# Batch 0's low-rank mixing in four partial sums at full array height, 58 instead of 62 unread matmuls, batch 1's values in two parts

## The chip, the cores and the metric

One core of a Trainium2 chip. The metric is the device time of one execution in microseconds (us), median over repeated executions. TensorE is called PE, its weight loads PEld, VectorE DVE, ScalarE ACT, GpSimd POOL, SyncE SP, as in the profile.

## The reference

Sliding-window attention with a window of 64 over 8 batches, 8 heads, 576 positions, 64 dimensions; then a token mixing of rank 32 and an MLP:

```python
scores = np.where(mask, scale * np.matmul(q, k.transpose(0, 1, 3, 2)), -1e9)   # window 64
x = softmax(scores) @ v                      # heads side by side: [8, 576, 512]
u = x + ((x.transpose(0, 2, 1) @ U) @ V).transpose(0, 2, 1)     # rank 32
out = u + np.maximum(u @ w_ch1, 0.0) @ w_ch2                    # 512 -> 2048 -> 512
```

## The kernel before

One instruction stream per engine. While the MLP of one chunk of 512 tokens runs on PE (`psA` is its first layer, `psU` its second), pieces of the next batches' attention are put between its matmuls at slots of a table. Four places matter here. The start keeps PE busy while the first inputs load, with matmuls whose results nobody reads ("unread"):

```python
def turn_over(n, cols, rows=P):
    for _ in range(n):
        nc.tensor.matmul(unread[0:rows, 0:cols], idle[:, 0:rows], idle[:, 0:cols], start=True, stop=True)
turn_over(62, 96)
```

Each of these pairs is a weight load and a matmul, two PE instructions. Then batch 0's attention: transposes of k and q (`tpm`, `tpg`), scores (`sc`), values (`xh`, `xr`), and its mixing. `UM` makes x U in four groups of 32 output rows, `HT` and `VM` multiply by V:

```python
for g in (t % 2, t % 2 + 2):                                  # UM, steps t = 0 to 3
    nc.tensor.matmul(hh["ps"][g * R : (g + 1) * R, :], ub[odd][:, t, :], xt, start=(t < 2), stop=False)
...
half = slice(n * 2 * R, (n + 1) * 2 * R)                      # VM: 64 of the 128 rows
nc.tensor.matmul(ps[0][n], vrep[half, off : off + P], hh["sb"][half, lo : lo + cols], start=True, stop=True)
```

Batch 1's values (`PVA`) are one piece of 72 matmuls at slot 20. VectorE then normalises them (`xs`), and batch 1's mixing (`pshh`) at slot 25 waits for that. The second weight matrix `w2b` is loaded in four quarters. Batch 0 has `spare=True`, the others not.

The softmax here doesn't subtract the row's maximum and nothing guards it: scores larger than these inputs give would overflow.

## Time and profile before

| | before |
|---|---|
| median of three executions | 312.85 us (312.75 to 312.92) |
| the profiled execution | 313.08 us, span 311.4 us |
| PE busy | 98% of the span |
| batch 0's U, last step / first `psA` of its MLP | 19.21 / 21.80 us |
| batch 1's mixing starts | 51.61 us |
| last quarter of `w2b` lands | 47.7 us |

The times within the span are read from the timeline of PE. After batch 1's mixing PE runs through almost without a wait, so a shift of PE at 51.61 us is a shift of the end, unless something later takes it back.

### The profile page before, as it was taken

To read this page: it belongs to the slowest core of one execution; us is meant where nothing else is said; L and a number is where in the kernel's file an instruction comes from. 1 tells how busy PE (TensorE), PEld (TensorE's weight loads), DVE (VectorE), ACT (ScalarE), POOL (GpSimd) and SP (SyncE) were. 2 spreads that over 40 slices of the span, in tenths; PEclk is the share of its full clock that TensorE was granted. 3 is DMA by queue.
4 is the path that set the end of the run, shared out by engine and by line. 5 is a ranking of instruction groups with operands and counts; after the bars stand their busy time and mean duration, and the time that the engine had idled before them with its cause. 6 is when DMAs were issued, how large, how long until landed. Compare 5 with 4: busy or idle time off the path is not lost.

```text
span 311.4 us, 6970 instructions
## 1 busy us (share of the span) xinstructions
PE 303.9 (98%) x2897; PEld 148.4 (48%) x2919; DVE 161.8 (52%) x308; ACT 108.8 (35%) x173; POOL 101.7 (33%) x133
## 2 busy tenths in 40 slices
PE   8989999999999999999999999999999999999996
PEld 7643554544455544453445344544454444444443
DVE  4665467437758753774368435844574343016011
ACT  3745670467038510642063304340345003201500
POOL 8693263293497097029308710000000000000000
PEclk9999999999999999999999999999999999999999
DMA  7999999999999999999999999515100545010012
GB/s 108 167 210 208 205 168 147 145 148 154 129 150 140 126 152 156 182 161 159 163 155 207 150 106 181 128 48 133 69 2 0 120 180 193 27 76 34 0 64 73
DMA packets 156496, 39.88 MB, mean 128 GB/s; under 512 B 145040, under 2 KB 151440, under 8 KB 156464
## 3 DMA queue, kind: packets, MB, share of 16 engines
q0 software_dynamic: 104720, 18.88, 87.3%
q1 hardware_dynamic: 51744, 20.55, 35.0%
q8 instruction: 23, 0.38, 0.5%
q14 instruction: 9, 0.07, 0.1%
HBM read 37.97 MB, written 9.44 MB: 152 GB/s over the span
## 4 chain that ended last, share of the span: by engine, by line
PE 93%; DMA 3%; POOL 2%; issue 1%; ACT 0%; DVE 0%; POOLq 0%
PE psA L724 41%; PE psU L748 40%; DMA vA<-in_v_dram 3%; PE sc L345 3%; PE xw L407 2%; PE psv L619 2%; PE pshh L531 1%; PE tpu L653 1%; PE tpg L281 0%; POOL qr L119 0%; PE low L345 0%; PE psh L531 0%; POOL vB L151 0%; PE xr L407 0%; POOL kr L119 0%
## 5 line engine op out<-in xcount | busy, mean ns | idle before, releaser
L724 PE MATMUL psA<-uTc,w1b 128*128 128x512 bf16 (+1 forms) x580 | 131.2, 378 | 0.4 <-ACT uTc L599 0.4
L748 PE MATMUL psU<-w2b,c 128*128 128x512 bf16 (+2 forms) x572 | 127.5, 373 | 1.3 <-issue 0.3
L748 PEld LDWEIGHTS <-c 128*128 128x128 bf16 x592 | 56.0, 98 | 66.4 <-issue 3.6
L724 PEld LDWEIGHTS <-w1b 128*128 128x128 bf16 x580 | 54.1, 98 | 64.4 <-issue 2.9
L736 ACT ACTIVATE c<-psA 128x512 bf16<-128x512 f32 x84 | 50.0, 597 | 88.3 <-PE psA L724 88.0
L761 DVE TENSOR_TENSOR osb<-psU,un 128x512 f32<-128x512 f32 (+2 forms) x29 | 19.5, 672 | 69.3 <-PE psU L748 69.3
L734 DVE TENSOR_SCALAR c<-psA 128x512 bf16<-128x512 f32 x60 | 41.3, 688 | 25.6 <-PE psA L724 25.6
L634 DVE TENSOR_TENSOR un<-psv,xs 128x512 bf16<-128x512 f32 (+3 forms) x48 | 26.1, 592 | 23.5 <-PE psv L619 23.3
L365 ACT ACTIVATE pts<-sc 128x1024 bf16<-128x1024 f32 x32 | 31.4, 1028 | 2.3 <-PE sc L345 2.3
L137 POOL DMA_DIRECT2D vA<-in_v_dram x32 | 28.5, 915 | 8.1 <-DMA w1b<-in_moe_w_ch_dram 2.8
L128 POOL DMA_DIRECT2D qr<-in_q_dram x30 | 26.7, 890 | 4.5 <-DMA w2b<-in_moe_w_ch_dram 3.1
L128 POOL DMA_DIRECT2D kr<-in_k_dram x30 | 26.7, 890 | 4.1 <-PE psA L724 2.0
L398 ACT ACTIVATE ptl<-low 128x256 bf16<-128x256 f32 x6 | 2.3, 384 | 62.0 <-PE high L345 62.0
L371 DVE TENSOR_TENSOR pts<-pts,maskA 128x1024 bf16<-128x1024 bf16 x28 | 19.1, 682 | 1.7 <-ACT pts L365 1.7
L922 POOL COPY held<-qf 1x1 bf16<-1x1 bf16 x5 | 1.1, 228 | 54.0 <-DMA qf<-qr 54.0
L498 DVE TENSOR_TENSOR xs<-xw,rcw 128x896 bf16<-128x896 f32 x14 | 15.3, 1091 | 0.5
L345 PEld LDWEIGHTS <-kf 64*64 64x64 bf16 x704 | 9.9, 107 | 7.7 <-issue 7.0
L345 PE MATMUL sc<-qf,kf 64*64 64x128 bf16 (+1 forms) x608 | 11.7, 212 | 0.5 <-DVE qf L298 0.3
L407 PEld LDWEIGHTS <-pts 128*64 128x64 bf16 x512 | 9.9, 110 | 3.7 <-issue 3.2
L546 ACT CAST hh<-pshh 128x512 bf16<-128x512 f32 x7 | 4.1, 586 | 13.7 <-PE pshh L539 13.5
L656 ACT COPY uTc<-tpu 128x512 bf16<-128x512 bf16 x9 | 5.3, 585 | 10.2 <-PE tpu L653 10.2
L407 PE MATMUL xw<-vA,pts 128*64 128x65 bf16 x217 | 8.4, 195 | 0.0
(115 smaller groups left out, 175.3 us busy)
## 6 DMA issues: line engine op xcount, KB each, us to landing
out_dram<-osb SPq DMA_DIRECT2D x27, 256.0 KB, 2.3
vA<-in_v_dram POOLq DMA_DIRECT2D x32, 128.0 KB, 8.1
kr<-in_k_dram POOLq DMA_DIRECT2D x24, 128.0 KB, 5.8
qr<-in_q_dram POOLq DMA_DIRECT2D x24, 128.0 KB, 6.4
w2b<-in_moe_w_ch_dram POOLq DMA_DIRECT2D x4, 512.0 KB, 15.0
out_dram<-late SPq DMA_DIRECT2D x8, 256.0 KB, 3.0
vB<-in_v_dram POOLq DMA_DIRECT2D x8, 128.0 KB, 12.3
w1b<-in_moe_w_ch_dram POOLq DMA_DIRECT2D x2, 512.0 KB, 11.5
```

Source lines behind the costliest of these rows:

```text
L128: nc.gpsimd.dma_start(out=dst[0:rows, t, :, :], in_=src[b, :, t * P : t * P + rows, :].rearrange("h p d -> p h d"),)
L137: nc.gpsimd.dma_start(out=dst[:, :, 0:D], in_=v[b, :, lo : lo + P, :].rearrange("h p d -> p h d"))
L345: nc.tensor.matmul(sc[g][r0 : r0 + W, col * W : (col + n) * W], keys_of(j, u, rs), queries_of(j, blk, n, rs), start=not spare, stop=last o ...
L365: nc.scalar.activation(out=dst, in_=sc[:], func=ACT.Exp, scale=scale)
L371: nc.vector.tensor_tensor(out=dst, in0=dst, in1=maskA.rearrange("p g n w -> p g (n w)"), op=ALU.mult)
L407: nc.tensor.matmul(dst, pts[:, h // 2, h % 2, blk, :] if blk < NB - 1 else ptl[:, h // 2, h % 2, :], rhs, start=True, stop=True,)
L634: nc.vector.tensor_tensor(out=u_tiles[g][rs, cs], in0=ps[0][n][rs], in1=x[rs, t, :, :].rearrange("p h d -> p (h d)")[:, cs], op=ALU.add,)
L724: nc.tensor.matmul(ps[i][:, ts.start * P : ts.stop * P], w1b[:, dc, i * P : (i + 1) * P], uTc[:, ts, dc, :], start=(dc == 0), stop=(dc == ...
L734: nc.vector.tensor_relu(out=c1[i][:], in_=ps[i][:])
L736: nc.scalar.activation(out=c1[i][:], in_=ps[i][:], func=ACT.Relu)
L748: nc.tensor.matmul(acc[t][:, lo:hi], c1[i][:, t * P : (t + 1) * P], w2b[:, i, lo:hi], start=(i == 0), stop=(i == NFC - 1),)
L761: nc.vector.tensor_tensor(out=osb[:, lo:hi], in0=acc[t][:, lo:hi], in1=u_tiles[g][:, lo:hi], op=ALU.add,)
```

## The change

It is a local tuning of three places: batch 0's mixing gets matmuls of full array height in place of pairs of small tiles, the start gets fewer unread matmuls of slightly more columns, and batch 1's values are cut in two so that VectorE can begin to normalise sooner. The core of the diff, with cuts:

```diff
-    turn_over(62, 96)
+    turn_over(58, 102)
...
-                        for g in (t % 2, t % 2 + 2):
+                        for g in (t,) if spare else (t % 2, t % 2 + 2):
-                                start=(t < 2), stop=False,
+                                start=(t < 2 or spare), stop=False,
...
-                        cols = slice((g % 2) * CH // 2, (g % 2 + 1) * CH // 2)
+                        n = NFULL if spare else 2
+                        cols = slice((g % n) * CH // n, (g % n + 1) * CH // n)
...
-                        hh["sb"][half, dc * P : (dc + 1) * P],
-                        vrep[half, W : W + CH],
+                        hh["sb"][:, dc * P : (dc + 1) * P],
+                        vrep[:, W : W + CH],
...
-                    half = slice(n * 2 * R, (n + 1) * 2 * R)
+                    half = slice(0, P) if spare else slice(n * 2 * R, (n + 1) * 2 * R)
...
-        pcs["PV"] = [PVA] if not spare else ...
+        pcs["PV"] = [PVA] if b > 1 else [lambda: PVA((0,), False), lambda: PVA((1,))] if b == 1 else ...
...
-        "SV": [18, 18, 19, 19],
-        "PV": [20],
+        "SV": [18, 18, 19, 21],
+        "PV": [20, 22],
```

Inside `PVA` the loops over `n` now run over the part's `ns`, and the tail (`rest`, `one`) belongs to the second part. I call the three parts the start, the mixing and the split.

## The prediction

> **What bounds the kernel now.** I read the page first: who is busy, and what the chain that ended last is made of.
>
> ```profile
> span 311.4 us, 6970 instructions
> PE 303.9 (98%) x2897; PEld 148.4 (48%) x2919; DVE 161.8 (52%) x308; ACT 108.8 (35%) x173; POOL 101.7 (33%) x133
> ...
> PEclk9999999999999999999999999999999999999999
> DMA  7999999999999999999999999515100545010012
> ...
> PE 93%; DMA 3%; POOL 2%; issue 1%; ACT 0%; DVE 0%; POOLq 0%
> ```
>
> TensorE (PE) is busy 98% of the span at full granted clock, and 93% of the chain is PE. What is not PE is 3% DMA, 2% POOL and 1% issue, near the start. Next the table of who waited for whom on PE; it is seven rows long, and these are the ones inside the parts that change:
>
> ```profile
> PE unread L829 <- DVE idle L155: 1.3, 1, 1.3
> PE psA L724 <- ACT uTc L599: 0.4, 1, 0.4
> PE psh L539 <- issue: 0.4, 1, 0.4
> PE psU L748 <- issue: 0.3, 2, 0.2
> ```
>
> All seven add up to 3.1 us, 1.0% of 311.4. So the change, which touches three short places (the start, batch 0's mixing, batch 1's values), is about tenths of a microsecond; 2% would be 6.3 us. To place the tenths I read the timeline of PE around these places.
>
> ```profile
> 1.26 5.03 PE L829 MATMUL unread<-idle 128*128 128x96 bf16 x62 [1.26 <-DVE idle L155]
> ...
> 19.21 0.39 PE L531 MATMUL psh<-xs,ub 128*32 128x512 bf16 x2
> 19.97 0.29 PE L539 MATMUL psh<-xs,ub 128*32 128x256 bf16 x4 [0.36 <-issue]
> ...
> 21.80 1.89 PE L724 MATMUL psA<-uTc,w1b 128*128 128x512 bf16 x8 [0.40 <-ACT uTc L599]
> 23.62 0.39 PE L619 MATMUL psv<-hh,vrep 64*128 64x512 bf16 x2
> 23.94 1.04 PE L724 MATMUL psA<-uTc,w1b 128*128 128x512 bf16 x4
> ...
> 46.96 0.29 PE L407 MATMUL one<-vA,pts 128*64 128x65 bf16 x8
> 47.41 4.26 PE L748 MATMUL psU<-w2b,c 128*128 128x512 bf16 x19 [0.16 <-issue]
> 51.61 0.62 PE L531 MATMUL pshh<-xs,ub 128*32 128x512 bf16 x8
> ```
>
> Batch 1's values run from 45.90 (their first row) to 47.06 (start of the last), 72 matmuls at 16.4 ns, then second-layer matmuls (psU), then batch 1's mixing (pshh) at 51.61. The 0.16 us of idle before psU at 47.41 is probably not real: the weight loads restart at 47.18, and the page counts 22 fewer matmuls than loads, so a first psU at 47.20 is missing from the records. Two more lines matter, from the timeline of POOL and the table of DMA issues of 34 to 40 us: the last quarter of the second weight matrix.
>
> ```profile
> 35.68 0.75 POOL L243 DMA_DIRECT2D w2b<-in_moe_w_ch_dram  x1 [1.17 <-DMA w2b<-in_moe_w_ch_dram]
> ...
> w2b<-in_moe_w_ch_dram POOLq DMA_DIRECT2D x1, 512.0 KB, 12.0
> ```
>
> It lands at 35.68 + 12.0 = 47.7, with the DMA engines at 9 in all slices since about 8 us. Its issue waited for an earlier transfer, not for PE. This is a clock that does not move when PE gets faster.
>
> **What the Trainium skill says.** "TensorEngine Tiling (Array Packing)", Key Properties: changing the tiling mode, not merely the tile, drains TensorE. The trace agrees: a full-height 512-column matmul takes 13.81/64 = 0.216 us in the long psA runs, but the stretch from 21.80 to the psA at 27.28 holds 20 psA and three 64-row groups and takes 5.48 us; 5.48 - 20 x 0.216 = 1.17 us for the three groups, which concurrent matmuls of 512, 512 and 256 columns would fill for only 0.54. "TensorE: Matmul & The Clock Gate", Part 3, says tiles in different row or column groups run concurrently, some 4 ns apart. The trace agrees: the pairs of 32-column matmuls (L531) cover 0.39 us, one psU 0.38. Part 1 of that page says the clock is halved until about 3.4 us of sustained work. The trace shows 62 matmuls of 96 columns at 80 ns (4.96/62), and 96-column transposes at about 40 ns a pair right after 6.22: the switch falls just where these matmuls end. "Runtime: NRT & Kernel Launch", Instruction fetch mechanics, says instructions come in 16 KiB blocks of 256, mostly hidden; the page's 23 instruction packets of 0.38 MB agree in size, no view ties a wait to one.
>
> **The change part by part.**
>
> Start: 62 x 96 becomes 58 x 102 columns, 5952 becomes 5916. At 80 ns per 96 columns (0.83 ns each) that is 0.03 us less. It is worth nothing: the chain here runs through the load of v to 14.0 us and POOL's copies to 16.07. Eight instructions fewer, though.
>
> Batch 0, U: five steps. In four, two concurrent matmuls become one; since the second was free, about 0. In the last, four concurrent matmuls go from 256 to 128 columns: 128/512 x 0.216 = 0.05 us saved, on the path (it leads to hh, uTc, and the first psA at 21.80). HT: two concurrent pairs become four in turn; the first psA waits only for the copy of the first, so 0. The 0.36 us of issue before L539 (0.43 after what a normal follow-on would be, since 19.21 + 0.32 = 19.53) is not explained by its semaphore: the DVE result was ready at 19.2. If it is an instruction block arriving, the 16 instructions fewer before it move it to a place where PE waits for ScalarE anyway, and up to 0.43 us is won.
>
> Batch 0, V: three groups at 1.17 us become 4 x 0.216 + 2 x 0.109 = 1.08: 0.09 us saved. Sum of the front, called G: 0.14 us, or 0.57 if the issue wait goes.
>
> Batch 1's values: 28 matmuls at 45.90 - G, then 4 psU, then 4 psU that are the first to use the last quarter of w2b, then the other 44 values, then 12 psU, then the mixing. Before, all 72 stood ahead, so those psU ran at 47.20 + 4 x 0.216 = 48.06, 0.3 us after the landing. Now they are reached at 45.90 - G + 28 x 0.0164 + 0.12 (return to the full array, 47.06 + 0.016 to 47.20) + 0.86 = 47.34 - G, which is before 47.7. So PE waits until about 47.78, whatever G is. From there: 4 psU 0.86, switch 0.09, 44 values 0.72, switch 0.12, 12 psU 2.59, switch 0.09: mixing could start at 52.25, against 51.61, that is +0.64.
>
> VectorE adds to this. Before, its normalising took from 47.17 to 51.34 (4.2 us) and PE came at 51.61. Now one of the two large pieces (0.26 + 1.01 us) runs early, but the rest, 0.21 + 0.35 + 0.26 + 1.01 + 0.20 + 0.86 = 2.89 us, starts only after the second part. PE's stretch from the last value matmul to the mixing shrinks from 4.55 to 4.55 - 8 x 0.216 = 2.82, so PE waits some 0.2 us more. Sum: +0.64 + 0.2 = +0.84. Everything after is PE one to one, as the waits table shows no wait after 51.6. G is swallowed by the landing.
>
> **The rivals.** (1) The weights are no bound: landing is earlier in most executions, or the wait is short. Then the split costs only the extra switch, 0.21, and the VectorE wait 0.2, and gains G: +0.4 - 0.57 = -0.1 to -0.2 at best, +0.3 with G = 0.14. Against it: the landing is set by engines that are full. For it: only one execution was traced, and the repeats agree to 0.17 us, so a landing that shifts by tenths would not show. (2) The change was tuned on the chip, and gains I do not see exist: mode changes that the fewer tiles avoid at U, an instruction stall that goes, another one at 47 us that the split removes. If the 0.16 us idle were real and both stalls went, 0.6 to 0.8 us less: about 312.1. For it: the odd 58 x 102 and the shifted slots look chosen by measurement. (3) The clock: with fewer unread matmuls TensorE might stay at half clock a further window of 3.4 us; but that stretch ends on the load of v, so at most about 1 us more. Against it: the busy time is the same within 0.03 us. (4) Batch 0's split to full height makes V slower, as two matmuls in turn replace two at once; the drain, measured above, pays for it.
>
> **Range and chances.** My working gives 312.85 + 0.84 = 313.7. I take 313.5 for the weight of rivals 1 and 2. The range is 312.4 to 314.1: rival 1 at its good end (-0.2, and a little of rival 2) to my sum plus 0.4 for a landing that comes later. 2% is 6.3 us, twice all of PE's waits, so faster by that has 0.005 and slower 0.01; within 2% has 0.985.
>
> **What would show it right or wrong.** Right: the chain of waits has a DMA w2b piece near 47 to 48 us and PE a wait of 0.4 to 1.0 us on it before psU; a wait of pshh for VectorE of about 0.2; the first psA 0.05 to 0.5 us before 21.80; the later parts shifted by under 1 us and nothing else changed. Wrong: no wait on w2b (then rival 1); the 0.36 us issue wait at psh still there (then G is 0.14); transposes after 6.2 us at double time (rival 3); psv groups longer than 0.43 us (rival 4). A landing well before 47 us, or gains in a place I called free, would make the prediction wrong.

## The result, and the profile after

The change measured 314.54 us (314.00 to 316.00, six executions) beside 312.88 us for the kernel before (312.75 to 313.72). The ratio is 1.0056, 95% interval 1.0030 to 1.0081: inside the 2% band, but slower, and outside the predicted range of 312.4 to 314.1. Ratios here are the mean time of one kernel's fast runs over that of the other's of the same rounds, so not quite the ratio of the medians. Two of the six executions had a granted clock of 0.993 and 0.994 (315.43 and 316.00 us); the median of the other four is 314.19 us. So some 0.35 of the 1.66 us is that, and 1.3 us are left.

The page of the profiled execution (314.82 us, the longest of the four at full clock) answers to the first view of the prediction:

```profile
span 313.1 us, 6953 instructions
PE 304.5 (97%) x2888; PEld 148.8 (48%) x2911; DVE 162.9 (52%) x308; ACT 108.8 (35%) x173; POOL 101.5 (32%) x133
...
PE 93%; DMA 2%; DVE 2%; issue 1%; ACT 0%; POOL 0%; POOLq 0%
```

PE's busy time is the same within 0.6 us; the span grew by 1.7. So PE waits more. These are the new rows in the table of PE's waits (engine, what waits, what it waited for: us in total, times, longest):

```profile
PE sc L345 <- issue: 1.1, 1, 1.1
PE tpm L281 <- DMA qr<-in_q_dram: 0.4, 1, 0.4
...
PE tpg L281 <- DMA kr<-in_k_dram: 0.2, 1, 0.2
PE pshh L536 <- DVE xs L515: 0.2, 1, 0.2
```

The predicted wait for VectorE before `pshh` is there with its 0.2 us. The predicted wait for `w2b` is not. The largest is one that nobody predicted: 1.1 us of "issue", that is, idle time that no semaphore explains. The 0.4 us of `issue` before batch 0's U that the prediction speculated on is gone, as is the wait of the first `psA` for ACT. In the timeline of PE (start, length, line, work, and idle before it), first the row of the kernel before, then the changed one:

```profile
13.30 0.58 PE L345 MATMUL sc<-qf,kf 64*64 64x128 bf16 x18
```

```profile
13.59 0.60 PE L335 MATMUL sc<-maskB,ident 128*128 128x512 bf16 x2
14.12 0.28 PE L345 MATMUL sc<-qf,kf 64*64 64x128 bf16 x5
15.54 0.36 PE L345 MATMUL sc<-qf,kf 64*64 64x128 bf16 x13 [1.15 <-issue]
...
21.14 0.39 PE L536 MATMUL psh<-xs,ub 128*32 128x512 bf16 x1
21.18 0.40 PE L545 MATMUL psh<-xs,ub 128*32 128x128 bf16 x4
...
23.11 1.89 PE L729 MATMUL psA<-uTc,w1b 128*128 128x512 bf16 x8
...
53.34 0.62 PE L536 MATMUL pshh<-xs,ub 128*32 128x512 bf16 x8 [0.17 <-DVE xs L515]
```

The stall cuts one loop of 18 equal score matmuls after the fifth. Before, the same 18 ran in the one row of 0.58 us. Nothing in the source distinguishes matmul 5 from matmul 6, and batch 0's scores are not touched by the change. The first `psA` comes at 23.11 instead of 21.80 us and the mixing at 53.34 instead of 51.61: +1.73 us, as much as the whole difference of the spans.

**What stops PE in the middle of a loop.** I counted PE's instructions in program order and matched the weight loads in the trace to them by their order. The stall stands ahead of instruction 450, the 0.4 us stall of the kernel before ahead of instruction 706, which is 450 + 256. The Trainium skill ("Runtime: NRT & Kernel Launch", Instruction fetch mechanics) says PE's instructions arrive in blocks of 256, 16 KiB each, mostly hidden. The page shows packets of kind `instruction` on queue 8: 23 of them, 0.38 MB, so 16 KB each; PE's 2897 matmuls and 2919 weight loads would fill 22.7 such blocks. The DMA view of a window tells when one was under way. Of the kernel before, 10.9 to 12.0 us:

```profile
DMA packets 1274, 0.18 MB, mean 160 GB/s; under 512 B 1273, under 2 KB 1273, under 8 KB 1273
q8 instruction: 1, 0.02, 5.5%
```

Of the changed kernel, 12.7 to 14.1 us (its windows 9 to 10.9 and 10.9 to 12.0 us show no row of queue 8):

```profile
DMA packets 1533, 0.21 MB, mean 153 GB/s; under 512 B 1526, under 2 KB 1532, under 8 KB 1532
q8 instruction: 1, 0.02, 5.8%
```

So the block that begins with instruction 450 came in from 10.94 to 11.90 us before, and from 12.74 to 14.04 us after; PE reached the end of the block before it at 13.31 and 14.16 us, and went on at 13.47 and 15.54 us. (These are starts of weight loads, 1.39 us apart; the row of waits counts from the modelled end of the last matmul and so has 1.1.) In every trace of this case in which PE stood at this boundary, it went on 1.5 to 1.9 us after the packet's end. This is the account of the front of this execution: k and q landed later than in the kernel before, so the first scores start at 9.96 us instead of 9.14 (+0.82); the stall is 1.39 us instead of 0.16 (+1.23); from there to U's last step 0.12 us are gained on balance, from U's last step to the first `psA` 0.62, and in V 0.04. The sum is +1.27, and PE is 1.27 us late at the fourth group of `psA` (28.55 against 27.28). The experiments ask three things: which part of the change makes the packet late, what the other parts do alone, and whether the delays add.

### The profile page after: what moved, and what is told of

The parts are those of the page before. It is cut to its first block, busy times and chain, and to the rows that moved or that the text cites.

```text
span 313.1 us, 6953 instructions
## 1 busy us (share of the span) xinstructions
PE 304.5 (97%) x2888; PEld 148.8 (48%) x2911; DVE 162.9 (52%) x308; ACT 108.8 (35%) x173; POOL 101.5 (32%) x133
## 4 chain that ended last, share of the span: by engine, by line
PE 93%; DMA 2%; DVE 2%; issue 1%; ACT 0%; POOL 0%; POOLq 0%
PE psA L729 41%; PE psU L753 39%; PE sc L345 3%; PE xw L407 2%; DMA qr<-in_q_dram 2%; PE psv L624 2%; PE pshh L536 1%; PE tpu L658 1%; PE tpg L281 1%; PE low L345 0%; PE tpm L281 0%; PE sc L335 0%; PE psh L536 0%; DVE xs L418 0%; DVE xs L502 0%
## 5 line engine op out<-in xcount | busy, mean ns | idle before, releaser
L552 ACT CAST hh<-pshh 128x512 bf16<-128x512 f32 x7 | 4.1, 585 | 14.1 <-PE pshh L545 14.0
L766 DVE TENSOR_TENSOR late<-psU,un 128x512 f32<-128x512 f32 x8 | 5.4, 689 | 6.1 <-PE psU L753 6.0
```

Source lines behind the costliest of these rows:

```text
L766: nc.vector.tensor_tensor(out=osb[:, lo:hi], in0=acc[t][:, lo:hi], in1=u_tiles[g][:, lo:hi], op=ALU.add,)
```

## The experiments

Theory A: the start's eight PE instructions fewer move the block boundaries, the block at 450 is fetched late, and that delay lies beside the wait for `w2b`, which the split brings. The rivals: the mixing makes the loss; the loss is a chance of this execution, late inputs for instance; or the delays add (theory B).

### One part at a time

The start alone:

```diff
-    turn_over(62, 96)
+    turn_over(58, 102)
```

> The kernel before with 58 x 102 in place of 62 x 96 unread matmuls, nothing else. Theory F (instruction blocks): both traces have a PE stall that no semaphore explains at the same two program positions, instructions 450 and 706, exactly 256 apart (before: 0.16 us at 450 in batch 0's scores, 0.43 us at 706 before the last U step; after: 1.39 us at 450, none left at 706). Eight instructions fewer move which work stands there. If this shift alone causes the large stall: about +1.2 us in the scores, minus up to 0.43 at U, so +0.8 us, 313.7. Rival J (the loads of k and q just landed later in the profiled run, by chance): no slower, 312.4 to 312.9. Rival C (the clock of TensorE rises later because of fewer matmuls): first transposes at double time.

Measured 313.78 us against 313.03, ratio 1.0026 (1.0009 to 1.0042); without its one execution at a clock of 0.995 the median is 313.71. Its table of waits has this new row, beside 1.1 us for a late load of k, and the `issue` before U is gone:

```profile
PE sc L345 <- issue: 0.7, 1, 0.7
```

Its block 450 was fetched from 12.14 us, as late as in the full change, and PE stood from 13.83 to 14.78. So a change of instruction count that removes 0.03 us of work costs about 0.75 us.

The mixing alone (the hunks of `UM`, `HT` and `VM`, with 62 pairs and the values in one part):

```diff
-                        for g in (t % 2, t % 2 + 2):
+                        for g in (t,) if spare else (t % 2, t % 2 + 2):
```

> The kernel before with batch 0's mixing in four partial sums alone; position 450 keeps its work, 706 moves by eight instructions to the transposes behind the last U step. F: no large stall at 450, the 0.43 us before the last U step goes or hides, V gains some 0.05: 312.2 to 312.5. Rival: the mixing itself is slower (HT's four matmuls in turn): 313 or more.

Measured 312.82 against 313.03, ratio 0.9992 (0.9980 to 1.0004): the mixing is not the loss, and that rival falls. From the last full step of U to the first `psA` it takes 1.97 us (19.21 to 21.18) where the kernel before takes 2.59; but the start-only kernel, with the old mixing and its block boundary elsewhere, takes 2.04 (20.38 to 22.42). So 0.07 us of this is the mixing and 0.55 us the old stall at instruction 706, which is gone here.

That stall belongs to the one trace of the kernel before, though. Three traces below (the split alone, twice, and the split at slots 20 and 21) have the same PE instructions up to this point and take 2.19, 2.04 and 2.04 us for the stretch. In the first of them U's last step starts 0.36 us after the step before it and has no `issue`, where the kernel before takes 0.76 us and has 0.36 of it:

```profile
19.09 0.39 PE L536 MATMUL psh<-xs,ub 128*32 128x512 bf16 x2
19.45 0.29 PE L544 MATMUL psh<-xs,ub 128*32 128x256 bf16 x4
```

So the 0.55 us are not a gain that every execution has. From the first `psA` to the fourth group's, the V stretch, 5.48 us become 5.43 (21.18 to 26.61). PE is 0.68 us early at 45 us; 0.20 us of it are lost where the last quarter of `w2b` is first used, and 0.33 at the values of a later batch, near 102 us. So a gain ahead of a fixed landing is partly lost at the landing.

The split alone (62 pairs, old mixing):

```diff
-        "SV": [18, 18, 19, 19],
-        "PV": [20],
+        "SV": [18, 18, 19, 21],
+        "PV": [20, 22],
```

> The kernel before with batch 1's values in two parts alone. Switching cost and VectorE wait, as the trace of after has them: +0.2 and +0.2, so 313.3. The prediction's step (PE waits for the last quarter of w2b, landing at 47.7): +0.84, 313.7, with a wait of psU of about 0.4 us near 47.4. F: no instruction moves before the values, so the front is as before.

Measured 313.93 against 313.03, ratio 1.0026 (1.0014 to 1.0038). The timeline of PE has the wait the prediction described:

```profile
45.95 1.04 PE L753 MATMUL psU<-w2b,c 128*128 128x512 bf16 x4
47.78 1.02 PE L753 MATMUL psU<-w2b,c 128*128 128x512 bf16 x4 [0.79 <-DMA w2b<-in_moe_w_ch_dram]
...
52.51 0.61 PE L536 MATMUL pshh<-xs,ub 128*32 128x512 bf16 x8 [0.17 <-DVE xs L515]
```

The mixing starts at 52.51, 0.90 us later than before, and the median is 0.90 us over; the prediction's sum was 0.84. What the chain after the landing is made of, I read below from a run of the full change.

The full change without the split (the start and the mixing):

```diff
-        "SV": [18, 18, 19, 21],
-        "PV": [20, 22],
+        "SV": [18, 18, 19, 19],
+        "PV": [20],
```

> The kernel after with batch 1's values in one part again. F with the shift as cause: the 1.4 us stall in the scores stays, 314.54 - 0.4 = 314.1. If instead the split carries the loss: 312.3.

Measured 313.70 against 313.03, ratio 1.0020 (1.0008 to 1.0032), with 1.0 us of issue stall at instruction 450. PE did not wait for k or q in its trace, as in the kernel before, and it stalled all the same. So late inputs are not what makes the stall.

The mixing and the split, with 62 pairs (the full change less the start):

```diff
-    turn_over(58, 102)
+    turn_over(62, 96)
```

> The kernel after with the 62 x 96 unread matmuls of before put back (four partial sums and split kept). The split alone took 313.93 with PE waiting 0.8 us for the last quarter of w2b. If that landing is the clock, the 0.6 us that the mixing gains in front is swallowed whole: 313.9, with a wait on w2b of about 1.3 us. If gains simply add: 312.82 + 0.9 = 313.7 at most, 313.3 with the mixing's full front gain and no longer wait.

Measured 314.28 against 313.00, ratio 1.0036 (1.0012 to 1.0060). One execution ran at a clock of 0.995; without it the median is 314.22. No stall at 450, but the time of the full change all the same. This surprised me: `w2b` landed at 48.12 us in its trace, 0.4 us later than in the kernel before, and the mixing started at 52.88. The long wait for `w2b` that I expected is in no row of its table of waits, because k, q and the copies of v came late in this execution (0.7, 0.8 and 0.7 us of waits) and PE was hardly early. Taking one of two delays away gained little, because the other was waiting behind it.

### Is it the number of instructions?

To tell count from columns, the full change without the split, with the same unread columns in 62 pairs:

```diff
-    turn_over(58, 102)
+    turn_over(54, 102)
+    turn_over(8, 51)
```

> The kernel with four partial sums and unsplit values, with 54 x 102 and 8 x 51 unread matmuls: the 5916 columns of after, but 62 instructions pairs as before. F (position in the instruction stream): block 450 is fetched from about 10.9 us as with 62, the stall in the scores is 0.2 us or less, 312.8. If the number of columns or the width of 102 is the cause: a stall of about 1 us and 313.7.

Measured 313.13 against 313.00, ratio 0.9992 (0.9972 to 1.0013). The same mixing and the same 5916 unread columns as the kernel without the split, in eight instructions more: 0.13 us over before where that one was 0.67 over. Its block was fetched from 10.89 to 11.88 us and PE did not stop. The count it is.

Other counts, with the new mixing and no split: 66 x 90, 60 x 99, 59 x 101, and 60 x 99 again.

```diff
-    turn_over(62, 96)
+    turn_over(66, 90)      # the others: (60, 99), (59, 101)
```

> Four partial sums alone with 66 x 90 unread matmuls, so eight instructions more ahead. F: the block is fetched early as with 62 (usable near 13.3 us), but instruction 450 now belongs to the scores before, reached near 12.6 us, so PE stalls some 0.6 to 0.7 us there; 313.2 to 313.5. If only fewer instructions than 62 pairs hurt by chance of the loads: no stall, 312.8.

> Four partial sums alone with 60 x 99. The wait for the load of q stands 11 instructions ahead of the block's end (194) with 62 pairs, 15 with 60, 19 with 58. If the fetch is asked for when a fixed distance ahead of the waiting instruction is reached, and that distance is 16, then early fetch, no stall, 312.8; if it is 12, late fetch, stall of about 1 us, 313.7.

> Four partial sums alone with 59 x 101: the wait for q stands 17 instructions ahead of the block's end. With 15 the fetch was early (10.0 us), with 19 late (11.9 to 12.7). If the distance is 16: late, 12 us, a stall of about 1 us in the scores, 313.6. If it is 17 or 18: early, no stall, 312.9.

> Four partial sums alone with 60 x 99, timed longer, as the candidate that beats both: early fetch, no stall; 312.5 to 312.9, 0.1 to 0.4 under before; the front gain of 0.6 us is cut by the landing of w2b near 47.7 us.

Measured: 66 pairs 312.99 against 313.00, ratio 0.9999 (0.9971 to 1.0028), with 0.39 us at the boundary where I expected 0.6 to 0.7; 60 pairs 312.93, ratio 0.9997 (0.9968 to 1.0026), and the second time 313.14 against 312.97, ratio 1.0001 (0.9987 to 1.0015); 59 pairs 314.17, ratio 1.0036 (1.0011 to 1.0062), of whose four executions two ran at a clock of 0.994, and the two at full clock took 313.3 us. So the stall of 59 pairs, 0.9 us in the trace below, goes with only some 0.3 us of loss. None beats the kernel before. The second profile of 60 pairs fell on an execution of 314.07 us whose cause is another: q came late,

```profile
PE tpg L281 <- DMA qr<-in_q_dram: 1.3, 1, 1.3
```

with no issue stall. So one profile can show a late input and look like a slower kernel; the median of its five did not follow it.

Block 450 in all 18 traces, sorted by the number of pairs, worked out from the packets of queue 8 and the order of the weight loads. "To the end" is how many instructions lie between PE's wait for q's load and the last instruction of the block that PE was in when the packet started (the block ends at 194); "lag" is from PE's first weight load of the block 194 to 449 to the packet's start.

```
pairs  to the end  kernel                  lag   landed  PE at the boundary  goes on
66        3        mixing                 2.35   11.19        12.69           13.08
62       11        before                 3.01   11.90        13.31           13.47
62       11        mixing                 2.97   11.79        13.51           13.51
62       11        split                  2.21   11.32        13.38           13.39
62       11        split, again           2.64   12.06        13.87           13.88
62       11        mixing, split          1.81   11.61        14.23           14.23
62       11        mixing, split, again   2.36   11.86        13.85           13.85
62       11        padded                 2.19   11.88        14.07           14.07
62       11        split at 20 and 21     1.96   11.34        13.79           13.80
60       15        mixing                 1.82   10.99        13.56           13.58
60       15        mixing, again          2.62   11.76        15.19           15.21
59       17        mixing                 3.52   12.82        13.60           14.50
58       19        start                  4.16   13.27        13.83           14.78
58       19        without split          3.71   13.18        13.55           14.78
58       19        without split, again   3.39   13.02        13.74           14.77
58       19        full                   3.91   14.04        14.16           15.54
58       19        full, again            3.24   12.87        13.85           14.51
58       19        full, third            3.59   13.12        13.73           14.79
```

With 60 pairs or more the packet lands by 12.1 us and PE stands at most 0.4 us; with 59 or 58 it lands at 12.8 us or later and PE stands 0.66 to 1.39 us. There is no overlap in 18 traces. The count decides, and in these traces it decides between 59 and 60. That PE's sequencer looks some 16 instructions ahead, and asks for the next block only when this look-ahead gets past the wait for q, would fit the column "to the end"; it is an inference. The runs with 60 and 59 pairs came out as it was written down for a look-ahead of 16, but no run moves the wait without the count.

### What the split costs, and where

The split with its second part at slot 21 instead of 22, old mixing, 62 pairs:

```diff
-        "PV": [20],
+        "PV": [20, 21],
```

> The kernel before with batch 1's values in two parts with one step of second-layer matmuls between them, both ahead of the first use of the last quarter of w2b. One switch to the 64-column tiles and back more: +0.2 us, 313.2, no wait on w2b and none of pshh for VectorE. If splitting itself costs the 0.9 us of the split alone: 313.9.

Measured 313.18 against 312.97, ratio 1.0011 (0.9998 to 1.0023). Its mixing starts at 51.57 us, as before. So cutting the values in two costs little; it is the later slot (and with it the fourth `SV`, at 19 again here), which puts four `psU` of the last quarter ahead of the second part, that costs most of the 0.9 us.

The full change again, unaltered:

> The kernel after, unchanged, once more beside the others. The block of instruction 450 is fetched from 11.9 to 12.7 us as in the three traces with 58 pairs, PE stalls 0.7 to 1.4 us there, and the split adds 0.4 to 0.5 on top of what that kernel without the split took (313.70): 314.1 to 314.5. If the first profile of after was a chance of late loads: 313.5 or less.

Measured 314.12 against 312.97, ratio 1.0034 (1.0022 to 1.0047), five executions between 314.04 and 314.20. Its profiled execution is one of them, and its page has a different chain from the first one's:

```profile
PE 85%; DMA 11%; DVE 2%; POOL 1%; issue 1%; POOLq 0%
PE psU L753 37%; PE psA L729 36%; DMA w2b<-in_moe_w_ch_dram 9%; DMA vf<-in_moe_V_dram 2%; PE sc L345 2%; PE xw L407 2%; PE unread L834 2%; PE psv L624 1%; PE pshh L536 1%; PE tpu L658 1%; POOL vrep L223 1%; DVE qf L298 0%; PE low L345 0%; DVE xs L502 0%; PE sc L335 0%
```

The landing of `w2b` is on the path that ends last, so what PE lost before it, 0.23 us by the fourth group of `psA`, is not. The pieces of that chain, in order of time:

```profile
36.09 11.72 DMA w2b<-in_moe_w_ch_dram
47.81 0.04 issue
47.85 1.04 PE psU L753 x4
48.89 0.02 issue
48.92 0.69 DVE late L766
...
50.45 1.09 DVE xs L502
...
52.10 0.44 DVE xs L515
52.53 0.04 issue
52.58 0.61 PE pshh L536 x8
```

From the landing to the mixing it is 4.77 us: four `psU`, then VectorE's sum for the output that they complete (0.69 us, `late`), and behind it all of VectorE's normalising of the second part. The same 4.77 us stand in the split alone (47.74 to 52.51) and in the mixing with the split (48.12 to 52.88, 4.76). The prediction had the same 4.7 us by adding PE's work and a wait of 0.2; the chain shows that after the landing it is VectorE that sets the pace.

### Do the delays add?

After these twelve runs it was open whether the late block and the wait for `w2b` add up in the full change. So the full change, the one with 62 pairs, the one without the split, and the split alone ran once more, all four on one chip with five rounds. No edit is new:

```diff
 full change:           turn_over(58, 102), new mixing, "PV": [20, 22]
 with 62 pairs:         turn_over(62, 96),  new mixing, "PV": [20, 22]
 without the split:     turn_over(58, 102), new mixing, "PV": [20]
 the split alone:       turn_over(62, 96),  old mixing, "PV": [20, 22]
```

> The full change for the third time, beside the three kernels that lack a part of it. If the late block and the w2b wait lie beside each other (theory A): within 0.3 us of the kernel with 62 pairs in this call, some 1.1 us over before; the trace shows either a w2b wait or an arrival after the landing, never both in full. If they add (theory B): 0.6 to 0.8 us over the kernel with 62 pairs.

> Mixing and split with 62 pairs, no late block. A: 1.0 to 1.3 us over before, mixing of batch 1 starts 4.8 us after the landing of w2b's last quarter. B: 0.6 to 0.8 us less than the full change.

> The full change without the split: the block is fetched late (0.5 to 1.3 us of issue stall at batch 0's scores), no w2b wait; 0.6 to 0.8 us over before under both theories, and under A 0.3 to 0.5 under the full change.

> The split alone: 0.9 us over before as the first time; if the mixing of batch 0 has a cost of its own once the split is there, 0.2 to 0.3 us less than the kernel with 62 pairs and both; if that difference was the landing of one call, the same as it within 0.15.

| kernel | median | over before (312.99) | ratio, 95% interval |
|---|---|---|---|
| full change | 314.30 | +1.31 | 1.0044 (1.0027 to 1.0061) |
| with 62 pairs | 314.13 | +1.14 | 1.0033 (1.0017 to 1.0049) |
| without the split | 313.88 | +0.89 | 1.0029 (1.0012 to 1.0046) |
| the split alone | 314.24 | +1.25 | 1.0032 (1.0016 to 1.0049) |

The full change is 0.17 us over the kernel with 62 pairs, where theory B wanted 0.6 to 0.8. A loss of 0.89 (0.82 without its one execution at a clock of 0.993; I expected 0.6 to 0.8) and one of 1.25 make 1.31 together, not 2.14: they lie beside each other. From five executions each that is not certain by itself: the two intervals overlap, and the means differ by 0.36 us, give or take some 0.5. But the earlier calls gave 1.15 us over before for the full change and 1.28 for the kernel with 62 pairs, and the traces below agree. My expectation for the split alone, 0.9 us again, missed: this time it was 1.25. It is level with the mixing and split together, so the mixing has no cost of its own there. Its profiled execution saw `w2b` land at 48.35 us.

Two traces show both ways of it. With 62 pairs PE is early and waits:

```profile
PE psU L753 <- DMA w2b<-in_moe_w_ch_dram: 0.9, 1, 0.9
```

The full change stalls 0.8 us at its block, PE gets to the last quarter after it has landed (47.44 us), does not wait for it, and pays in VectorE's chain instead: the mixing starts at 52.67, with 62 pairs at 52.81. That profiled execution was also the longest of its five, 315.14 us, for another wait later on, which in the other traces shows only once (0.3 us, with 60 pairs):

```profile
PE psA L729 <- DMA uTc<-un: 0.7, 1, 0.7
```

Over the seven traces with the split at slots 20 and 22, the start of batch 1's mixing is 0.90, 0.97, 1.06, 1.20, 1.27, 1.51 and 1.73 us later than in the kernel before. Their mean, 1.23, is about what the medians say. In each of the seven the mixing starts 4.7 to 4.8 us after the first `psU` on the last quarter, and that `psU` starts when `w2b` lands (five traces: 47.78 to 48.39 us) or, if PE comes later, when PE gets there (47.84 and 48.60 us, both of the full change). So the later of the two sets the start of the mixing.

## Why the prediction was wrong

**The start failed.** "It is worth nothing ... Eight instructions fewer, though" named the fact and gave it no weight. Alone the new start costs 0.75 us in the median, because the block of instructions at 450 is then fetched late and PE stands 0.7 to 1.4 us in batch 0's scores. The prediction had the mechanism in its hands one paragraph later, at U, and asked only whether the block boundary that it could see would move to a harmless place. It did. That another block's fetch would become late, it did not ask. For the start and the mixing together it had a gain of 0.14 or 0.57 us; measured was a loss of 0.67 and 0.89.

**In the full change the size of the split was off too.** The term of +0.84 for landing and VectorE measured 0.90 and 1.25 in the split alone, 1.28 and 1.14 with the mixing. Taking the start out of the full change gains 0.17 us (314.30 to 314.13), taking the split out 0.42 (to 313.88); with five executions each, these two differences are within the noise, so which error carries more of the miss stays open.

**So the front's G had the wrong sign.** It was put at 0.14 or 0.57 us of gain. In its trace the mixing alone gained 0.67 us in front, and taken apart, 0.07 at U and 0.05 at V are the mixing (predicted 0.05 and 0.09; the working's 1.17 us for the three groups is 1.16), 0.55 the stall at 706 that goes (predicted up to 0.43). The steps on the mixing were right within 0.04 us. The step on the stall fits the trace that it was read from, by luck: three other traces with the same instructions up to there have 0.15 us or nothing to gain. With the start, the front lost 0.23, 0.51 and 1.27 us in the three traces of the full change.

**"PE waits until about 47.78, whatever G is" holds only while G is a gain.** In the first trace PE came after the landing and there was no wait for `w2b`, one of the marks that I had named for being wrong. The second trace has the DMA piece in the chain that I had named for being right, but not the wait of 0.4 to 1.0 us: PE came only some 0.2 us before the landing. Both are the same kernel. The end is the later of two paths, and a loss on one is partly hidden by the other.

**The split was right in kind, and what was off in its size is the landing.** Its sum, 0.64 for the landing and 0.2 for VectorE, was 0.84; the first trace of the split alone showed 0.90, the wait of `pshh` for VectorE 0.2 in every trace. But 47.7 us came from one trace; over the traces here the landing lies between 47.3 and 48.4, and where PE is in time the mixing follows it one to one (47.74 to 52.51 and 48.35 to 53.12 in the two traces of the split alone). The allowance of 0.4 us for it in the range was too small, and it left no room for a late PE.

**The number was moved the wrong way.** The working gave 313.7, and 313.5 went on record for the weight of rivals 1 and 2. Neither came true as a gain: the weights did bound, and the odd 58 x 102, which I had read as a sign of tuning, gained nothing. The full change at full clock has medians of 314.19, 314.12 and 314.30; the record's 314.54 holds two executions at the lower clock on top. Rival 3 showed in small: in the first trace the first transposes run at their old rate (12 in 0.45 us), in the second the first two groups take 0.69 and 0.60 us instead of 0.45 and 0.42, which is 0.4 us, ahead of the landing and so hidden by it. Rival 4 had groups of 0.43 us for two full-height V matmuls in turn, just what was computed. That all of it stays within 2% held.

**Open.** Why PE asks for the block late (the look-ahead is an inference), and what makes the landing of `w2b` differ by a microsecond between executions. No version here beats the kernel before with an interval that excludes 1; the nearest is the mixing alone.

## What to carry to other kernels

Before you change the number of instructions ahead of a critical stretch, filler included, count where the engine's blocks of 256 end and, if the inference above holds, which wait stands in the last few instructions before the end of one: here, on PE, eight instructions of filler fewer cost 0.75 us. When two parts of a change both delay the same join, measure each alone and both together: here the two delays gave about the larger, not the sum, and undoing one of them gained only 0.17 or 0.42 us. Read a stall in more than one trace of the same instructions before you book it as a gain. And take a transfer's landing from several traces before a prediction leans on tenths of it.

## What the Trainium skill lacked or had wrong

- "Runtime: NRT & Kernel Launch", Instruction fetch mechanics, calls the crossing of a 16 KiB block mostly hidden. Here PE stood 0.7 to 1.4 us at one boundary in all seven traces with 58 or 59 pairs, and about 0.4 us at the next in the trace of the kernel before, against 0.15 us or less in three others with the same instructions up to there. The page gives no latency: the packet took 0.9 to 1.3 us, with the DMA engines busy 90% or more, and where PE stood at this boundary it went on 1.5 to 1.9 us after the packet's end.
- The same section has the next block fetched while the current one runs, but no page says when in it. Here it was 1.8 to 3.0 us after PE entered the block before with 60 pairs or more, and 3.2 to 4.2 us with 58 or 59, where the wait for q stands 17 or 19 instructions before that block instead of 15 or fewer.
- "TensorEngine Tiling (Array Packing)", Key Properties, names the drain at a change of mode without a size. Batch 0's V stretch gives one as an estimate: three groups took 1.16 us where their columns fill 0.54, so 0.62 us for six changes, 0.1 us each. Replacing them by full-height matmuls gained only 0.05 us, since these take twice the time.
